# Transposing attention probabilities with VectorE 32x32 blocks and SBUF-to-SBUF DMAs instead of TensorE

## The chip, the cores and the metric

The kernel runs on one NeuronCore of a Trainium2 chip. Five engines work side by side, each through its own instructions in the order in which they were written: TensorE (PE; its weight loads are listed apart as PEld), VectorE (DVE), ScalarE (ACT), GpSimd (POOL) and SyncE (SP), which here issues every DMA. They wait for one another through semaphores. The metric is the time of one execution on the device in microseconds; the time before is the median of three runs.

## The reference

First an attention in which keys and values are averaged over groups of eight positions, then a gated feed-forward block with four weight matrices, all in float32.

```python
B, H, S, D = 8, 8, 576, 64                      # q, k, v: (B, H, S, D)
k_p = k.reshape(B, H, 72, 8, D).mean(axis=3)    # 72 pooled keys for each head
v_p = v.reshape(B, H, 72, 8, D).mean(axis=3)
scores = q @ k_p.T / sqrt(D)
attn = softmax(scores)
attn_out = attn @ v_p                           # 4608 tokens x 512
x = attn_out.transpose(0, 2, 1, 3).reshape(4608, 512)
out = (((x @ w1) * (x @ w2)) @ w3) @ w_out      # 512 -> 1024 -> 1024 -> 512
```

The kernel first multiplies w3 by w_out into one 1024 x 512 matrix, and splits values into a high and a low part, so that three (in one place four) matrix products in a shorter format give the accuracy of float32.

## The kernel before

**Chunks and tiles.** The 4608 tokens are cut into 12 chunks of 384 (`CH`). A chunk that lies in one batch element has three tiles of 128 tokens; chunks 1, 4, 7 and 10 straddle two batch elements and have four tiles of 96 (`tok_tiles`). Attention runs on tiles, the feed-forward block on whole chunks. Attention of chunk n runs beside the feed-forward block of chunk n - 1.

**One order for all engines.** Nothing is planned by costs. `at(kind, k, fn, ...)` (L599) notes a function with a slot number k; at the end (L722) the list is sorted by whole slot, then kind in the order L (loads), P (work on VectorE, ScalarE and GpSimd), M (feed-forward products), A (attention products), then the fraction of the slot, then the order of noting, and is written out. Each engine has its own instructions in just this order; the engines may be apart from one another by as much as the semaphores allow. SyncE has most of its slots empty and often runs far ahead.

**A chunk's 24 slots.** The feed-forward block of chunk m begins at slot m0. For each of eight column blocks j it takes three slots: at 3j the product with w1 (`a_mm`, L525, PSUM bank a), at 3j+1 the product with w2 (`b_mm`, bank b), and at 3j+5, so one block later, the product with the merged matrix (`out_mm`, L560). Between them, ScalarE copies a out of PSUM (`a_post`, slot 3j+1), VectorE multiplies b by it and ScalarE rounds the result to its high part gh (`b_post`, slot 3j+2), and VectorE makes the low part gl (`g_lo`, slot 3j+2.5). Banks a and b exist once each: the next `a_mm` needs `a_post`, the next `b_mm` needs `b_post`, and `out_mm` needs gl from its third matmul on. After the last block the result goes out through `out_post` (slot 27, so slot 3 of the next chunk), one of its three copies on VectorE (L572) and each followed by a store on SyncE (L575).

**A tile's attention.** `s_mm` (L404, two halves, slots s and s+1) makes the scores; `soft1` to `soft3` (slots s+1 to s+3) make exp, sum, division, and R, a small tile with the high and low parts of eight of the 72 columns; `pt_mm` and `ptr_mm` (L464, L474) transpose the probabilities E and the tile R on TensorE into PSUM, four and two 128-column pieces; one slot later `pt_post` (L486, L487) splits the result into PTh and PTl, and `ptr_post` (L491) copies PTr. When all tiles of the chunk are done, `av_mm` (L499 to L502) multiplies by the pooled values, one pair of heads at a time, and `av_post` leaves the feed-forward input xT. Attention uses three PSUM banks (tag att).

**Slots before, counted from m0 of the chunk that runs beside.** Chunk 2 and later, three tiles: s = 0, 3, 6; transposes at 5, 8, 11; `av_mm` at 15 to 18. Four tiles: s = 0, 3, 6, 9; transposes at 6, 9, 12, 15; `av_mm` at 17 to 20.

**Loads around it.** For chunk n + 1, q comes in during slots 6 to 9, one pair of heads in each (`load_q`, L265): four DMAs of 48 KB per pair, or, if chunk n + 1 straddles two batch elements, eight of 24 KB; every packet has 128 bytes. VectorE transposes q in 32x32 blocks (`tr_q`, L276, slots 15 to 18). Some chunks also load k (slots 8, 10, 12, 14; L307) and v (L343, L356). All these go through SyncE, and each of its instructions waits there until the buffer it writes is free.

Of the kernel before, what the change touches and what calls it, by code (L numbers as in the profile page):

```python
# [8 lines left out]
F32 = mybir.dt.float32  # L9
F32R = mybir.dt.float32r  # L10
# [8 lines left out]
def kernel(  # L19
# [14 lines left out]
    nc = tc.nc  # L34
# [3 lines left out]
    P = 128  # L38
# [3 lines left out]
    KR = KP - KM  # L42
# [7 lines left out]
    CH = 384  # L50
# [37 lines left out]
    def f(ap):  # L88
        return ap.bitcast(F32)
# [65 lines left out]
    def w_tiles(s):  # L155
        if s == 0:
            stage["wt"] = [t[:, i] for t, x in (
                (p1.tile([P, x, 512], I32, tag=tag, name="wt"), x)
                for tag, x in (("PTh", 3), ("PTl", 3), ("PTr", 1))) for i in range(x)]
        if s < NJ:  # L160
            stage["wo", s] = stage["wt"][s % 4], f(stage["wt"][4 + s % 3])
        stage["w3", s] = W_cell(0, 4 + s % 4, I32), W_cell(1, 4 + s % 4, F32)
# [85 lines left out]
    def tok_tiles(n):  # L248
        res = []
        for (b, s0, cnt, off) in pieces(n):  # L250
            step = 128 if cnt == 384 else 96
            for x in range(0, cnt, step):
                res.append((b, off + x, step))
        return res
# [137 lines left out]
            nc.gpsimd.tensor_tensor(  # L392
                out=VR[b % 2][rows, r // 2::2, D * par:D * par + D], in0=hi[rows], in1=m[rows], op=ALU.add)

    Et, Mt, PTh, PTl, PTr, xT = {}, {}, {}, {}, {}, {}

    Sp = {}

# [46 lines left out]
    def soft3(n, t):  # L445
        b, off, nt = tok_tiles(n)[t]
        E = Et[n, t]
        R = Rt[n, t] = p2.tile([P, NPR, 2, 2, 2, KR], F32R, tag="R", name="R")
        er = E[:nt].rearrange("p (a h) (x e) -> p a (h x) e", h=2, e=KR)[:, :, 0:18:17, :]
        for dup in range(2):  # L450
            nc.scalar.copy(out=R[:nt, :, :, dup, 0], in_=er)
        for dup in range(2):
            nc.vector.tensor_tensor(
                out=R[:nt, :, :, dup, 1], in0=er, in1=f(R[:nt, :, :, dup, 0]), op=ALU.subtract)
# [13 lines left out]
    def ptr_mm(n, t):  # L468
# [6 lines left out]
                out=rv[:, g, :nt], in_=R[:nt, g * P:(g + 1) * P], identity=ident[:nt, :nt])  # L475
        Tp[n, t, "r"] = rv

    def pt_post(n, t):
        b, off, nt = tok_tiles(n)[t]
        if t == 0:  # L480
            PTh[n] = p1.tile([P, NPR, CH], F32R, tag="PTh", name="PTh")
            PTl[n] = p1.tile([P, NPR, CH], F32R, tag="PTl", name="PTl")
            PTr[n] = p1.tile([P, 2, CH], F32R, tag="PTr", name="PTr")
        pv = Tp.pop((n, t))
        hi, lo = PTh[n][:, :, off:off + nt], PTl[n][:, :, off:off + nt]
        nc.scalar.copy(out=hi, in_=pv[:, :, :nt])  # L486
        nc.vector.tensor_tensor(out=lo, in0=pv[:, :, :nt], in1=f(hi), op=ALU.subtract)  # L487

    def ptr_post(n, t):
        b, off, nt = tok_tiles(n)[t]  # L490
        nc.scalar.copy(out=PTr[n][:, :, off:off + nt], in_=Tp.pop((n, t, "r"))[:, :, :nt])  # L491

    def av_mm(n, pr):
        ps = patt.tile([P, 512], F32, tag="att", name="att")
        for (b, s0, cnt, off) in pieces(n):
            c = slice(off, off + cnt)
            vh, vl = (vbd[b % 2][s][:, pr] for s in range(2))
            o = ps[:, c]
            nc.tensor.matmul(out=o, lhsT=vh, rhs=PTh[n][:, pr, c], start=True, stop=False)  # L499
            nc.tensor.matmul(out=o, lhsT=vh, rhs=PTl[n][:, pr, c], start=False, stop=False)  # L500
            nc.tensor.matmul(out=o, lhsT=vl, rhs=PTh[n][:, pr, c], start=False, stop=False)  # L501
            nc.tensor.matmul(out=o, lhsT=VR[b % 2][:, pr], rhs=PTr[n][:, pr // 2, c], start=False, stop=True)  # L502
        Tp[n, pr, "x"] = ps

    def av_post(n, pr):
# [93 lines left out]
    def at(kind, k, fn, *args):  # L599


        plan.append((k // 1, "LPMA".index(kind), k % 1, len(plan), fn, args))

    def plan_att(n, s_at, ds, pt_at, av_at):


        for t in range(len(tok_tiles(n))):
            for half in range(2):
                k = s_at[t] + ds * half
                at("A", k, s_mm, n, t, half)  # L610
                at("P", k + 1, soft1, n, t, half)
            at("P", k + 2, soft2, n, t)
            at("P", k + 3, soft3, n, t)
            k = pt_at[t]
            at("A", k, pt_mm, n, t)
            at("A", k, ptr_mm, n, t)
            at("P", k + 1, pt_post, n, t)
            at("P", k + 1, ptr_post, n, t)
        for pr in range(NPR):
            at("A", av_at[pr], av_mm, n, pr)  # L620
            at("P", av_at[pr] + 1, av_post, n, pr)
# [81 lines left out]
    for n in range(1, NCH):  # L703
        k = M0 + 3 * NJ * (n - 1)
        nt = len(tok_tiles(n))
        s0, pt, av = (3, 5.5, 20.5) if n == 1 else (0, 6, 17) if nt == 4 else (0, 5, 15)
        s_at = [k + s0 + 3 * t for t in range(nt)]
        plan_att(n, s_at, 1, [x + pt for x in s_at], [k + av + pr for pr in range(NPR)])
        if n == 1:
            plan_q3(n, [K0 + 8.5 + 1.5 * pr for pr in range(NPR)], [K0 + 12, K0 + 13, K0 + 15, K0 + 15.5])  # L710
        else:
            plan_q(n, k - 18, 1, k - 9, 1)
# [41 lines left out]
```

## Time and profile before

| | |
|---|---|
| median of three runs | 807.89 us (807.57 to 809.64) |
| span of the profiled execution | 803.4 us; its own time isn't listed apart, so what lies around the span is taken as the median less the span, 4.5 us |
| TensorE busy | 777.9 us, 97% |
| TensorE weight loads | 722.2 us, 90% |
| VectorE / ScalarE / GpSimd | 54% / 36% / 24% |
| mean granted TensorE clock | 0.989 |
| DMA | 62.6 MB in 106,632 packets, 73,680 of them under 512 bytes |

Busy time of TensorE overlaps itself, since matmuls are pipelined; where one group of products really gives way to the next is better read from the start of its first weight load. The chain in part 4 of the page is followed back from the last instruction. In a timeline, a row gives the start in us, the duration, the engine and line, the operation with output and inputs, and how many were merged.

### The profile page before, as it was taken

What the parts mean: (1) busy time and instruction counts of PE and PEld (TensorE: products, weight loads), DVE (VectorE), ACT (ScalarE), POOL (GpSimd) and SP (SyncE); (2) the same over time, 40 slices, a digit from 0 to 9 for tenths busy, and PEclk for the clock granted to TensorE, in tenths of its full rate; (3) what the DMA queues carried; (4) which work ended last, traced back from release to release, by engine and by line L of the source; (5) the groups of instructions that cost most, each with busy time, mean ns of one, the idle gap of its engine ahead of it and who ended that gap; (6) DMA issues with size and microseconds to landing.
All of it is one profiled execution on the core that took longest, in us unless ns stands there. A gap on an engine that the chain in (4) does not pass through costs nothing.

```text
span 803.4 us, 11625 instructions
## 1 busy us (share of the span) xinstructions
PE 777.9 (97%) x4344; PEld 722.2 (90%) x4344; DVE 431.7 (54%) x873; ACT 288.0 (36%) x727; POOL 196.1 (24%) x234
## 2 busy tenths in 40 slices
PE   7899888999999999999999999999999999999998
PEld 6677777899999999999999999999999999999997
DVE  6968989465373375374374374474454455452112
ACT  5567565332243233242242333232242332332211
POOL 2155465107007302025008102034028020000000
PEclk8999999999999999999999999999999999999999
DMA  9988960045034030062043030071143110100101
GB/s 333 267 206 217 273 145 1 1 94 123 1 72 120 27 80 1 1 143 75 1 95 109 27 67 1 17 157 44 43 85 91 53 26 1 40 1 1 40 1 39
DMA packets 106632, 62.63 MB, mean 78 GB/s; under 512 B 73680, under 2 KB 90320, under 8 KB 106576
## 3 DMA queue, kind: packets, MB, share of 16 engines
q1 hardware_dynamic: 106576, 61.89, 30.1%
q8 instruction: 34, 0.56, 0.3%
q14 instruction: 22, 0.18, 0.1%
HBM read 52.43 MB, written 9.44 MB: 77 GB/s over the span
## 4 chain that ended last, share of the span: by engine, by line
PE 85%; DVE 7%; DMA 4%; issue 2%; ACT 2%; SPq 0%; DVEq 0%
PE o L560 24%; PE a L525 24%; PE b L525 23%; PE att L404 4%; PE o L586 2%; DMA st<-in_k_dram 2%; PE att L464 2%; DVE wb L140 1%; DVE wb L148 1%; PE att L501 1%; PE att L500 1%; PE att L502 1%; PE att L499 1%; PE att L474 1%; DMA raw<-in_moe_w_out_dram 1%
## 5 line engine op out<-in xcount | busy, mean ns | idle before, releaser
L525 PE MATMUL a<-xT,hl 128*128 128x384 f32 x1152 | 223.1, 342 | 0.0
L525 PE MATMUL b<-xT,hl 128*128 128x384 f32 x1152 | 220.3, 339 | 0.4 <-DVE Wc L153 0.4
L525 PEld LDWEIGHTS a<-xT,hl 128*128 128x128 f32 x1152 | 205.0, 190 | 4.9 <-POOL hl L153 0.2
L525 PEld LDWEIGHTS b<-xT,hl 128*128 128x128 f32 x1152 | 198.7, 188 | 0.8 <-DVE Wc L153 0.8
L560 PE MATMUL o<-Wc,gh 128*128 128x512 f32 x576 | 183.6, 400 | 0.0
L560 PEld LDWEIGHTS o<-Wc,gh 128*128 128x128 f32 x576 | 105.1, 189 | 17.3
L545 DVE TENSOR_TENSOR a<-b,a 128x384 f32<-128x384 f32 x96 | 53.1, 553 | 123.5 <-PE b L525 123.5
L362 POOL TENSOR_TENSOR st<-st 72x512 f32<-72x512 f32 (+1 forms) x53 | 73.0, 1377 | 173.2 <-DMA st<-in_k_dram 161.0
L560 PE MATMUL o<-Wc,gl 128*128 128x512 f32 x288 | 114.0, 396 | 0.0
L535 ACT COPY a<-a 128x384 f32<-128x384 f32 x96 | 46.1, 480 | 179.9 <-PE a L525 160.6
L546 ACT CAST gh<-a 128x384 fp32r<-128x384 f32 x96 | 49.2, 512 | 148.4 <-DVE a L545 148.4
L551 DVE TENSOR_TENSOR gl<-a,gh 128x384 fp32r<-128x384 f32 x96 | 59.4, 619 | 35.8 <-ACT gh L546 35.4
L375 POOL TENSOR_TENSOR vbd<-vm,vbd 64x256 fp32r<-64x256 f32 x16 | 13.3, 833 | 249.8 <-ACT vbd L374 248.2
L560 PEld LDWEIGHTS o<-Wc,gl 128*128 128x128 f32 x288 | 54.1, 188 | 12.5
L511 DVE TENSOR_TENSOR xT<-att,xT 128x384 fp32r<-128x384 f32 x48 | 26.5, 556 | 70.0 <-ACT xT L510 70.0
L426 DVE TENSOR_REDUCE sm<-E 128x4 f32<-128x288 f32 (+1 forms) x70 | 31.6, 451 | 46.3 <-ACT E L425 46.3
L404 PE MATMUL att<-kbd,qT 128*128 128x144 f32 (+1 forms) x320 | 52.1, 286 | 0.2 <-ACT E L430 0.2
L420 DVE TENSOR_REDUCE mx<-att 128x4 f32<-128x288 f32 (+1 forms) x80 | 36.0, 450 | 28.8 <-PE att L404 28.7
L425 ACT ACTIVATE E<-E 128x288 f32<-128x288 f32 (+1 forms) x70 | 31.1, 445 | 55.4 <-DVE E L422 55.4
L404 PEld LDWEIGHTS att<-kbd,qT 128*128 128x128 f32 (+1 forms) x320 | 46.6, 179 | 1.1 <-ACT E L430 0.5
L586 PE MATMUL o<-hl 128*128 128x512 f32 x144 | 42.3, 430 | 3.3 <-DVE hl L177 3.3
L363 POOL TENSOR_TENSOR st<-st 72x256 f32<-72x256 f32 (+1 forms) x53 | 41.8, 789 | 4.2
(87 smaller groups left out, 806.4 us busy)
## 6 DMA issues: line engine op xcount, KB each, us to landing
raw<-in_moe_w_dram SPq DMA_DIRECT2D x32, 512.0 KB
st<-in_k_dram SPq DMA_DIRECT2D x32, 288.0 KB
out_dram<-ob SPq DMA_DIRECT2D x35, 256.0 KB
st<-in_v_dram SPq DMA_DIRECT2D x32, 256.0 KB
qs<-in_q_dram SPq DMA_DIRECT2D x128, 48.0 KB
raw<-in_moe_w_out_dram SPq DMA_DIRECT2D x8, 512.0 KB
st<-in_v_dram SPq DMA_DIRECT2D x64, 64.0 KB
qs<-in_q_dram SPq DMA_DIRECT2D x96, 24.0 KB
```

The source lines that it names most:

```text
L362: nc.gpsimd.tensor_tensor(out=t[:, :, 0:4], in0=t[:, :, 0:4], in1=t[:, :, 4:8], op=ALU.add)
L363: nc.gpsimd.tensor_tensor(out=t[:, :, 0:2], in0=t[:, :, 0:2], in1=t[:, :, 2:4], op=ALU.add)
L404: nc.tensor.matmul(out=ps[:nt, 2 * KP * j:2 * KP * (j + 1)], lhsT=qT[n][:, pr, off:off + nt], rhs=kbd[b % 2][:, pr], start=True, stop=True,)
L420: nc.vector.tensor_reduce(out=mx[:nt, hs], in_=sv, axis=AX.X, op=ALU.min)
L426: nc.vector.reduce_sum(out=sm[:nt, hs], in_=E[:nt, hs], axis=AX.X)
L525: nc.tensor.matmul(out=o, lhsT=w12[j, w][sw][:, kt * P:(kt + 1) * P], rhs=x[sx][:, kt], start=(i == 0), stop=(i == 3 * NK - 1))
L535: nc.scalar.copy(out=a, in_=gt[m, j][:, :CH])
L545: nc.vector.tensor_tensor(out=g, in0=ps[:, :CH], in1=g, op=ALU.mult)
L546: nc.scalar.copy(out=gh, in_=g)
L551: nc.vector.tensor_tensor(out=gl, in0=g, in1=f(gh), op=ALU.subtract)
L560: nc.tensor.matmul(out=oacc[m][t], lhsT=(gh, gl)[sg][:, c], rhs=W[j][sw], start=(j == 0 and i == 0), stop=(j == NJ - 1 and i == 2))
L586: nc.tensor.matmul(out=wacc[h][it], lhsT=w3t[s][sa][:, it * P:(it + 1) * P], rhs=wo[j][sb], start=(j == 0 and i == 0), stop=(j == NJ - 1 a ...
```

## The change

From chunk 2 on, `pt_mm`, `ptr_mm`, `pt_post` and `ptr_post` aren't used. In their place stand three functions. `pt_turn` (slot s+4, VectorE) transposes E and R in 32x32 blocks into a tile T of 128 x 6 x 128. `pt_move` (slot s+5, SyncE) puts the blocks in their places with DMAs from T to the tile PTx: one for each 32 tokens and each 32 of the 128 target partitions, so 16 for a tile of 128 tokens and 12 for one of 96; each moves 32 partitions x 6 x 32 numbers, 24 KB in pieces of 128 bytes. `pt_split` (slot s+9) makes PTh on ScalarE and subtracts it on VectorE, in place in the first four parts of PTx; the last two parts of PTx take the place of PTr. T and PTx have one buffer each, and R now has one in place of two. The scores begin one slot earlier (s = -1, 2, 5 and, with four tiles, 8); `av_mm` is at 17 to 20, or at 18.5 to 21.5 with four tiles. Chunks 0 and 1 keep TensorE's transposes and write to the new tiles.

```diff
     def soft3(n, t):
         b, off, nt = tok_tiles(n)[t]
         E = Et[n, t]
-        R = Rt[n, t] = p2.tile([P, NPR, 2, 2, 2, KR], F32R, tag="R", name="R")
+        R = Rt[n, t] = p1.tile([P, NPR, 2, 2, 2, KR], F32R, tag="T" if (n, t) == (0, 1) else "R", name="R")
...
+    def pt_tiles(n):
+        PTh[n] = p1.tile([P, NPR, CH], F32R, tag="PTh", name="PTh")
+        PTx[n] = p1.tile([P, NPR + 2, CH], F32R, tag="PTx", name="PTx")
+
+    def pt_turn(n, t):
+
+        b, off, nt = tok_tiles(n)[t]
+        if t == 0:
+            pt_tiles(n)
+        E = Et[n, t].rearrange("p (a h) k -> p a (h k)", h=2)
+        T = Tp[n, t] = p1.tile([P, NPR + 2, P], F32, tag="T", name="T")
+        nc.vector.transpose(out=T[:nt, :NPR], in_=E[:nt, :, KR:KR + P])
+        nc.vector.transpose(
+            out=T[:nt, NPR:].rearrange("p a c -> p (a c)"),
+            in_=f(Rt[n, t][:nt].rearrange("p a h u s e -> p (a h u s e)")))
+
+    def pt_move(n, t):
+        b, off, nt = tok_tiles(n)[t]
+        T = Tp.pop((n, t))
+        for c in range(nt // 32):
+            for g in range(4):
+                nc.sync.dma_start(
+                    out=f(PTx[n])[32 * g:32 * g + 32, :, off + 32 * c:off + 32 * c + 32],
+                    in_=T[32 * c:32 * c + 32, :, 32 * g:32 * g + 32])
+
+    def pt_split(n, t):
+        b, off, nt = tok_tiles(n)[t]
+        hi, lo = PTh[n][:, :, off:off + nt], PTx[n][:, :NPR, off:off + nt]
+        split(f(lo), hi, lo)
+
...
             at("P", k + 2, soft2, n, t)
             at("P", k + 3, soft3, n, t)
+            if n > 1:
+                at("P", k + 4, pt_turn, n, t)
+                at("L", k + 5, pt_move, n, t)
+                at("P", pt_at[t], pt_split, n, t)
+                continue
             k = pt_at[t]
             at("A", k, pt_mm, n, t)
             at("A", k, ptr_mm, n, t)
...
-        s0, pt, av = (3, 5.5, 20.5) if n == 1 else (0, 6, 17) if nt == 4 else (0, 5, 15)
+        s0, pt, av = (3, 5.5, 20.5) if n == 1 else (-1, 9, 18.5) if nt == 4 else (-1, 9, 17)
         s_at = [k + s0 + 3 * t for t in range(nt)]
         plan_att(n, s_at, 1, [x + pt for x in s_at], [k + av + pr for pr in range(NPR)])
```

More of the change, by code (lines that the diff above doesn't have):

```diff
@@ L158, in w_tiles @@
                 (p1.tile([P, x, 512], I32, tag=tag, name="wt"), x)
-                for tag, x in (("PTh", 3), ("PTl", 3), ("PTr", 1))) for i in range(x)]
+                for tag, x in (("PTh", 3), ("PTx", 4))) for i in range(x)]
         if s < NJ:
@@ L393, in prep_vr2 @@
                 out=VR[b % 2][rows, r // 2::2, D * par:D * par + D], in0=hi[rows], in1=m[rows], op=ALU.add)
-    Et, Mt, PTh, PTl, PTr, xT = {}, {}, {}, {}, {}, {}
+    Et, Mt, PTh, PTx, xT = {}, {}, {}, {}, {}
     Sp = {}
@@ L480, in pt_post @@
         if t == 0:
-            PTh[n] = p1.tile([P, NPR, CH], F32R, tag="PTh", name="PTh")
-            PTl[n] = p1.tile([P, NPR, CH], F32R, tag="PTl", name="PTl")
-            PTr[n] = p1.tile([P, 2, CH], F32R, tag="PTr", name="PTr")
+            pt_tiles(n)
         pv = Tp.pop((n, t))
-        hi, lo = PTh[n][:, :, off:off + nt], PTl[n][:, :, off:off + nt]
+        hi, lo = PTh[n][:, :, off:off + nt], PTx[n][:, :NPR, off:off + nt]
         nc.scalar.copy(out=hi, in_=pv[:, :, :nt])
@@ L490, in ptr_post @@
         b, off, nt = tok_tiles(n)[t]
-        nc.scalar.copy(out=PTr[n][:, :, off:off + nt], in_=Tp.pop((n, t, "r"))[:, :, :nt])
+        nc.scalar.copy(out=PTx[n][:, NPR:, off:off + nt], in_=Tp.pop((n, t, "r"))[:, :, :nt])
     def av_mm(n, pr):
@@ L499, in av_mm @@
             nc.tensor.matmul(out=o, lhsT=vh, rhs=PTh[n][:, pr, c], start=True, stop=False)
-            nc.tensor.matmul(out=o, lhsT=vh, rhs=PTl[n][:, pr, c], start=False, stop=False)
+            nc.tensor.matmul(out=o, lhsT=vh, rhs=PTx[n][:, pr, c], start=False, stop=False)
             nc.tensor.matmul(out=o, lhsT=vl, rhs=PTh[n][:, pr, c], start=False, stop=False)
-            nc.tensor.matmul(out=o, lhsT=VR[b % 2][:, pr], rhs=PTr[n][:, pr // 2, c], start=False, stop=True)
+            nc.tensor.matmul(out=o, lhsT=VR[b % 2][:, pr], rhs=PTx[n][:, NPR + pr // 2, c], start=False, stop=True)
         Tp[n, pr, "x"] = ps
```

## The prediction

> **What bounds the kernel now.** I read first the page's busy times and its chain of waits.
>
> ```profile
> span 803.4 us, 11625 instructions
> PE 777.9 (97%) x4344; PEld 722.2 (90%) x4344; DVE 431.7 (54%) x873; ACT 288.0 (36%) x727; POOL 196.1 (24%) x234
> PE 85%; DVE 7%; DMA 4%; issue 2%; ACT 2%; SPq 0%; DVEq 0%
> DVE a L545 <- PE b L525: 123.5, 62, 5.0
> ```
>
> TensorE holds 85% of the chain, and VectorE mostly waits for it (fourth row, from the list of waits: 123.5 us before the product with b). So each TensorE instruction taken out is worth its own time, as long as nothing else gets late. What it is worth, and when TensorE needs what, stands in the timeline of weight loads beside chunk 3 (three tiles, 128 tokens), and at the end for a tile of 96:
>
> ```profile
> 401.83 2.17 PEld L525 LDWEIGHTS a<-xT,hl 128*128 128x128 f32 x12
> 403.99 0.60 PEld L404 LDWEIGHTS att<-kbd,qT 128*128 128x128 f32 x4
> 404.53 2.05 PEld L525 LDWEIGHTS b<-xT,hl 128*128 128x128 f32 x12
> ...
> 409.08 0.59 PEld L464 LDWEIGHTS att<-ident,E 128*128 128x128 f32 x4
> 409.64 0.25 PEld L474 LDWEIGHTS att<-ident,R 128*128 128x128 f32 x2
> 409.86 2.06 PEld L525 LDWEIGHTS a<-xT,hl 128*128 128x128 f32 x12
> ...
> 433.03 0.19 PEld L499 LDWEIGHTS att<-PTh,vbd 128*128 128x128 f32 x1
> ...
> 433.74 2.10 PEld L525 LDWEIGHTS b<-xT,hl 128*128 128x128 f32 x12
> ...
> 436.52 0.36 PEld L560 LDWEIGHTS o<-Wc,gh 128*128 128x128 f32 x2
> 436.93 0.19 PEld L560 LDWEIGHTS o<-Wc,gl 128*128 128x128 f32 x1
> ...
> 469.51 0.48 PEld L464 LDWEIGHTS att<-ident,E 96*128 96x128 f32 x4
> 470.10 0.49 PEld L404 LDWEIGHTS att<-kbd,qT 128*96 128x96 f32 x4
> ```
>
> **What it removes.** The six transposes of a 128-token tile take TensorE from 409.08 to 409.86, 0.78 us, those of a 96-token tile from 469.51 to 470.10, 0.59 us. Chunks 2 to 11 have 21 tiles of 128 (seven chunks) and 12 of 96 (chunks 4, 7, 10): 21 x 0.78 + 12 x 0.59 = 23.4 us. ScalarE loses the copies of PTr. The split stays, now out of SBUF; I keep its times. None of that is on the chain.
>
> **What it adds.** VectorE transposes 768 numbers per partition in two instructions. ScalarE's and VectorE's rows, grouped by shape:
>
> ```profile
> L276 DVE STREAM_TRANSPOSE qT<-qs 128x384 f32<-128x384 f32 x40 | 22.7, 568 | 0.0
> L486 ACT CAST PTh<-att 128x512 fp32r<-128x512 f32 x24 | 14.0, 583 | 17.3 <-PE att L464 17.3
> L487 DVE TENSOR_TENSOR PTl<-att,PTh 128x512 fp32r<-128x512 f32 x24 | 16.6, 690 | 12.5 <-ACT PTh L486 12.5
> L551 DVE TENSOR_TENSOR gl<-a,gh 128x384 fp32r<-128x384 f32 x96 | 59.4, 619 | 35.8 <-ACT gh L546 35.4
> ```
>
> 768 is twice 384, so 2 x 0.568 = 1.14 us per tile. VectorE is busy for 54% of the span, so its idle time covers that; without this cover it would be 33 x 1.14 = 38 us. R with one buffer, and scores a slot earlier, I cost at nothing: `pt_turn` has read R two slots before the next tile's R is written, and TensorE does the same scores. If R did make ScalarE wait, it would be for one `pt_turn`, 1.14 us a tile.
>
> The real cost is SyncE's. It must issue 16 (or 12) DMAs per tile, 48 per chunk in both kinds of chunk. Nothing in this trace moves SBUF to SBUF; SyncE's own timeline shows what issues cost otherwise:
>
> ```profile
> 404.05 11.89 SPq L265 DMA_DIRECT2D qs<-in_q_dram  x24
> ...
> 416.44 3.76 SPq L265 DMA_DIRECT2D qs<-in_q_dram  x8
> 420.30 0.79 SPq L307 DMA_DIRECT2D st<-in_k_dram  x2
> ...
> 436.50 5.40 SPq L356 DMA_DIRECT2D st<-in_v_dram  x8
> ...
> 462.30 9.54 SPq L265 DMA_DIRECT2D qs<-in_q_dram  x16
> ...
> 169.68 5.60 SPq L265 DMA_DIRECT2D qs<-in_q_dram  x11
> ```
>
> An issue costs 0.395 us at the least (k, 0.79 for two) and 0.675 at the most (v, 5.40 for eight). The nearest is q of chunk 4: 24 KB each, the same 32 partitions, six pieces and 128 bytes as the moves; 11.89/24 = 0.495 and 3.76/8 = 0.47. I take 0.485; for the 48 KB form 5.60/11 = 0.51. To see when the last lands, the DMA view of 462 to 474 us (40 slices of 0.3 us):
>
> ```profile
> qs<-in_q_dram SPq DMA_DIRECT2D x16, 48.0 KB
> DMA  1999999847548284654839457200008386472000
> ```
>
> SyncE ends the sixteenth at 462.30 + 9.54 = 471.84, so began it about 471.35; packets cease in slice 37, near 473.1: 1.75 us from issue to landing. A tile of 128 thus occupies SyncE for 16 x 0.485 = 7.76 us, and has landed 15 x 0.485 + 1.75 = 9.0 us after the first issue; a tile of 96 takes 5.8 and 7.1 us. TensorE reaches a next tile after three slots, some 7 us. And T has one buffer: the next `pt_turn` waits, on VectorE, for all 16 landings, with `soft1` of the next tile and `b_post` queued behind it; `pt_split` waits for them on ScalarE, with `a_post` behind it, and on VectorE with `g_lo` behind it.
>
> **The chain of one chunk.** Zero is the start of slot 3 (401.83 above). TensorE wants the fifth gl at its third matmul of slot 17: 436.93 - 401.83 = 35.1 us before the change, less three tiles' transposes (2.3), two `av_mm` that move behind it (433.03 to 433.74, 0.71 each) and one half of scores (403.99 to 404.53, 0.54): 30.8 us. `g_lo` of block 4 (slot 14.5) stands behind `pt_split` of tile 2 (slot 14) on VectorE. When is that ready? `pt_turn` 0 stands behind `out_post`'s copy:
>
> ```profile
> 402.47 0.68 DVE L572 COPY ob<-o 128x512 f32<-128x512 f32 x1
> ```
>
> so it ends near 403.15 + 1.14, at 2.5. SyncE's order is move 0, q pair 0, move 1, q pairs 1 to 3, move 2.
>
> Chunks 2, 5, 8 (next q: four 48 KB issues, 2.04 us, per pair): move 0 is issued 2.55 to 10.3 and landed at 11.6; q to 12.35; `pt_turn` 1 runs 11.6 to 12.75; move 1 12.75 to 20.5; q to 26.6; move 2 26.6 to 34.4, landed 35.65. Then the split's 0.58 + 0.69, `g_lo`'s 0.6 and 0.3 us that I allow for three handoffs: 37.8. Late by 7.0 us.
>
> Chunks 3, 6, 9 (next q: eight 24 KB issues, 3.9 us, per pair): q to 14.2; move 1 to 21.95; q to 33.6; move 2 to 41.35, landed 42.6; gl at 44.75. Late by 13.95.
>
> Chunks 4, 7, 10: move 0 2.5 to 8.35, landed 9.6; q to 10.4; `pt_turn` 1 to 10.7; move 1 to 16.55; q to 22.65; move 2 to 28.5, landed 29.75; `pt_turn` 3, planned for slot 12 (some 21), runs 29.75 to 30.85; move 3 to 36.7, landed 38.0, split done 39.3. `av_mm` wants it at 36.0: slot 17 starts at 30.4 and two more halves of scores (1.1), then come two products of some 2.2. Late by 3.3.
>
> Chunk 11 (no q after it): landings at 11.6, 21.8, 32.0; gl at 34.15. Late by 3.4.
>
> Sum of the stalls: 3 x 7.0 + 3 x 13.95 + 3 x 3.3 + 3.4 = 76.1 us. TensorE catches up nothing, since it is the bound between the stalls; SyncE does, as it now stands idle before the stores of a chunk for up to 54.7 us:
>
> ```profile
> SPq L575 <- ACT ob L574: 439.3, 12, 54.7
> ```
>
> The q and k loads that now stand behind moves still come in time: the last q pair is issued by 33.6, and `tr_q` of it stands in slot 18. Net +76.1 - 23.4 = +52.7: a span of 856.1, and with the 4.5 us between this span (803.4) and the median of the runs (807.89), 861 us.
>
> **Bounds.** With 0.395 us an issue, the same steps give stalls of 2.85, 9.8, 0 and 0: 38.0 in all, +14.6, 822 us. With 0.675: 15.75, 23, 11.8 and 11.8: 163.5, +140, 948 us. The middle price is kept because its DMAs have the same form and size as the moves; that the source is SBUF instead of DRAM is the open point.
>
> **Rivals.** *Hidden, faster.* If the issues cost little, only 23.4 us of TensorE go: 784.5. The place is the wait for move 2. By the steps above gl is ready at 15.4 + 46c (chunks 2, 5, 8) and 22 + 47c (3, 6, 9) for an issue price c, against 30.8. All is hidden for c below 0.19; the stalls equal the gain near c = 0.35, and below that the change wins. For it: VectorE's and the DMA engines' free time. Against it: no group of issues above is below 0.395. The Trainium skill, DMA: Bandwidth & Descriptors, Rules for kernel authors, says to issue a DMA early and wait late, so that its fixed cost overlaps compute; the five slots between `pt_turn` and `pt_split` do that for one tile, and by this rule alone the time would be this rival's. No row here bears it out for 48 issues in a row.
>
> *Cheap issues, slightly slower.* c between 0.36 and 0.43, as for k: by the same two lines, 812 to 837.
>
> *Packets, not issues, set the pace.* In the stretch of the 24 issues the DMA engines are busy a third of the time:
>
> ```profile
> 408.00:410.00 2.00, 2.00 (x14) 1.70 (x13) 1.45 (x4) 0.78 (x3) 0.00 (x0) 1.00 0.32 51
> ```
>
> 0.32 of 0.485 us is 0.155 us of packets per DMA. Were SBUF to SBUF packets over three times as slow, they would outlast the issue; at four times, 0.62 us a DMA, so some 921 us. The Trainium skill, DMA: Bandwidth & Descriptors, Specifications, says that below 512 bytes a DMA engine does read-modify-write; a doubling by that would stay hidden at a share of 0.64.
>
> **How the numbers follow.** A difference under 0.3% (2.4 us) can't be told from none. The forecast (c from 0.43 to 0.6, 837 to 911 us) gets 0.63; cheap issues 0.13; dearer issues or packets (over 911) 0.09; hidden or nearly so, 784 to 805, 0.12; a draw, with c at 0.35, 0.03. Slower is 0.63 + 0.13 + 0.09 = 0.85. The range, 806 to 925, leaves out the faster cases, part of the draw and the far end.
>
> **What would show it.** In the changed kernel: SyncE rows of 16 moves in about 7.8 us, back to back; VectorE idle before its transposes of tiles 1 and 2, ended by a DMA from T; ScalarE idle before the split of the last tile, 5 us and more; TensorE's gaps at the out product of slot 17, about 7 us beside chunks 2, 5, 8 and 14 beside chunks 3, 6, 9; granted clock unchanged. It would be wrong if an issue from SBUF costs under 0.35 us, if VectorE doesn't wait for T, or if TensorE's gaps stand elsewhere.

## The result, and the profile after

The changed kernel takes 977.64 us (971.9 to 980.32), the kernel before, run beside it, 808.45: a ratio of 1.211, 95% interval 1.205 to 1.218. The prediction had the sign and the bound right and the size wrong: 861 us, with a range to 925. The profiled execution has a span of 974.4 us where the prediction's sum gave 856.1, so 118 us have to be explained.

The page of the changed kernel (busy times, granted clock, chain of waits):

```profile
PE 814.7 (84%) x4146; PEld 741.6 (76%) x4146; DVE 451.0 (46%) x939; ACT 279.2 (29%) x694; POOL 193.1 (20%) x234
PEclk8999999889978989978977997987997897998999
PE 37%; SPq 32%; DVE 14%; DMA 8%; issue 5%; ACT 3%; DVEq 0%; ACTq 0%
```

TensorE held 85% of the chain before; now it holds 37% and SyncE's queue (SPq) 32%, of which 28 points are the one line that issues the moves. VectorE's busy time grows by 19 us only (451.0 against 431.7). The granted clock (PEclk, in tenths of full speed) falls in patches.

Its list of waits:

```profile
DVE T L489 <- DMA PTx<-T: 137.5, 23, 11.6
DVE PTx L153 <- ACT PTh L152: 129.2, 33, 14.1
PEld b L553 <- DVE a L573: 82.5, 18, 9.7
ACT PTh L152 <- DMA PTx<-T: 81.6, 10, 12.9
PEld o L588 <- DVE gl L579: 56.7, 15, 8.7
```

Before, VectorE waited for TensorE's b, and TensorE for hardly anything. Now the reverse has appeared: TensorE waits for VectorE's a and gl, VectorE for T or for ScalarE's PTh, and both for the moves. The prediction named these waits, but it looked for TensorE's gaps at gl and `av_mm` alone. The larger share stands before the product with b, at slots 10 and 13 of a chunk with three tiles: `b_post` is queued on VectorE behind the turn of the next tile, and that turn waits for T.

Chunk by chunk: the table of windows, before and after. Each row runs from the first product with w1 of one chunk to that of the next; the rows are those in which attention of chunks 3 and 4 runs beside (the same table has 58.11 us for chunk 2 and 57.94 for chunk 11). Columns: window, length, busy time of PE, PEld, DVE, ACT, POOL with counts, granted clock, DMA share, GB/s. Before, without a gap in TensorE's busy time:

```profile
218.31:276.56 58.25, 58.25 (x328) 54.92 (x326) 28.76 (x62) 19.12 (x47) 21.17 (x27) 1.00 0.29 75
276.56:336.31 59.75, 59.75 (x353) 56.38 (x352) 31.46 (x74) 19.39 (x51) 6.65 (x9) 1.00 0.12 27
```

After, chunks 2, 3, 4 and 11; where the busy time of PE is shorter than the window, TensorE stands idle:

```profile
163.26:239.05 75.79, 62.99 (x311) 58.08 (x310) 29.61 (x67) 16.98 (x40) 15.02 (x18) 0.89 0.36 73
239.05:321.35 82.30, 61.62 (x310) 56.46 (x309) 30.43 (x67) 18.32 (x44) 20.83 (x27) 0.90 0.33 68
321.35:391.83 70.48, 62.02 (x331) 56.19 (x330) 34.77 (x81) 18.82 (x47) 5.89 (x9) 0.95 0.21 40
849.74:917.77 68.03, 58.81 (x303) 54.25 (x302) 27.64 (x63) 15.91 (x37) 0.00 (x0) 0.95 0.14 30
```

The four kinds of chunk grow by 17.7, 24.1, 10.7 and 10.1 us, and TensorE, which had no gap, stands idle for 12.8, 20.7, 8.5 and 9.2 us. The prediction's net figures were 7.0 - 2.3, 13.95 - 2.3, 3.3 - 2.4 and 3.4 - 2.3, so 4.7, 11.6, 0.9 and 1.1: the order of the kinds is right, and each is about 9 to 13 us too small. The window after the last of these is as before (56.6 us both times): nothing is lost there, where there are no moves.

The chain that the prediction worked out, in the chunk that was hit worst, chunk 3. SyncE's own timeline, after:

```profile
250.11 10.44 SPq L499 DMA_DIRECT2D PTx<-T  x16
260.59 7.85 SPq L265 DMA_DIRECT2D qs<-in_q_dram  x16
268.55 10.33 SPq L499 DMA_DIRECT2D PTx<-T  x16
278.93 3.98 SPq L265 DMA_DIRECT2D qs<-in_q_dram  x8
283.01 0.36 SPq L307 DMA_DIRECT2D st<-in_k_dram  x1
283.41 4.28 SPq L265 DMA_DIRECT2D qs<-in_q_dram  x8
...
288.24 10.72 SPq L499 DMA_DIRECT2D PTx<-T  x16
```

From 250.11 to 298.96 the queue issues without a break. Sixteen moves take 10.3 us, 0.65 us each (10.33/16), where the prediction had 7.76. What follows the last move stands in three timelines of the same kernel: TensorE's weight loads (their first row is this chunk's zero, the start of slot 3), then ScalarE, then VectorE:

```profile
246.31 2.05 PEld L553 LDWEIGHTS a<-xT,hl 128*128 128x128 f32 x12
...
282.00 3.70 PEld L553 LDWEIGHTS b<-xT,hl 128*128 128x128 f32 x12 [9.46 <-DVE a L573]
...
302.20 0.29 PEld L588 LDWEIGHTS o<-Wc,gl 128*128 128x128 f32 x1 [8.70 <-DVE gl L579]
```

```profile
300.34 0.62 ACT L152 CAST PTh<-PTx 128x512 fp32r<-128x512 f32 x1 [12.91 <-DMA PTx<-T]
```

```profile
249.64 0.40 DVE L490 STREAM_TRANSPOSE T<-R 128x256 f32<-128x256 f32 x1
...
280.47 0.71 DVE L489 STREAM_TRANSPOSE T<-E 128x512 f32<-128x512 f32 x1 [11.39 <-DMA PTx<-T]
...
281.43 0.52 DVE L573 TENSOR_TENSOR a<-b,a 128x384 f32<-128x384 f32 x1
...
300.99 0.69 DVE L153 TENSOR_TENSOR PTx<-PTx,PTh 128x512 fp32r<-128x512 f32 x1 [14.11 <-ACT PTh L152]
```

The end is the chain as forecast: last move, landing, split on ScalarE and VectorE, the fifth gl, the out product of slot 17, which waited 8.70 us. But TensorE gets gl at 302.20 - 246.31 = 55.9 us, not 44.75. And it had stood 9.46 us before that, at 282.00: the turn of tile 2 waited 11.39 us for the moves of tile 1, and the product of b and a (281.43) stood behind it.

### The profile page after: what moved, and what is told of

It is laid out like the page before. It is cut to its first block, busy times and chain, and to the rows that moved or that the text cites. A ratio compares the mean times of both kernels' runs of the same rounds, so it can differ in the third digit from the quotient of the medians.

```text
span 974.4 us, 11953 instructions
## 1 busy us (share of the span) xinstructions
PE 814.7 (84%) x4146; PEld 741.6 (76%) x4146; DVE 451.0 (46%) x939; ACT 279.2 (29%) x694; POOL 193.1 (20%) x234
## 4 chain that ended last, share of the span: by engine, by line
PE 37%; SPq 32%; DVE 14%; DMA 8%; issue 5%; ACT 3%; DVEq 0%; ACTq 0%
SPq L499 28%; PE o L588 11%; PE b L553 9%; PE a L553 9%; DMA PTx<-T 5%; SPq L265 3%; PE o L614 2%; DMA qs<-in_q_dram 2%; DVE T L489 1%; PE att L404 1%; DVE mx L420 1%; DVE E L422 1%; ACT E L425 1%; DVE sm L426 1%; PE att L528 1%
## 5 line engine op out<-in xcount | busy, mean ns | idle before, releaser
L553 PE MATMUL b<-xT,hl 128*128 128x384 f32 x1152 | 247.1, 367 | 77.4 <-DVE a L573 76.8
L553 PEld LDWEIGHTS b<-xT,hl 128*128 128x128 f32 x1152 | 221.1, 208 | 83.4 <-DVE a L573 82.5
L553 PE MATMUL a<-xT,hl 128*128 128x384 f32 x1152 | 226.2, 345 | 1.1 <-ACT a L563 1.1
L588 PE MATMUL o<-Wc,gh 128*128 128x512 f32 x576 | 192.7, 417 | 1.1 <-ACT gh L574 1.1
L588 PE MATMUL o<-Wc,gl 128*128 128x512 f32 x288 | 122.6, 426 | 49.7 <-DVE gl L579 49.7
L588 PEld LDWEIGHTS o<-Wc,gh 128*128 128x128 f32 x576 | 115.0, 203 | 20.8 <-ACT gh L574 2.5
L588 PEld LDWEIGHTS o<-Wc,gl 128*128 128x128 f32 x288 | 58.3, 202 | 70.0 <-DVE gl L579 56.7
L574 ACT CAST gh<-a 128x384 fp32r<-128x384 f32 x96 | 49.2, 512 | 215.9 <-DVE a L573 215.9
L489 DVE STREAM_TRANSPOSE T<-E 128x512 f32<-128x512 f32 (+1 forms) x33 | 23.3, 707 | 137.5 <-DMA PTx<-T 137.5
L153 DVE TENSOR_TENSOR PTx<-PTx,PTh 128x512 fp32r<-128x512 f32 (+1 forms) x33 | 21.4, 649 | 129.2 <-ACT PTh L152 129.2
L579 DVE TENSOR_TENSOR gl<-a,gh 128x384 fp32r<-128x384 f32 x96 | 56.6, 589 | 15.5 <-ACT gh L574 14.8
```

Of the source, the lines that this page charges most:

```text
L553: nc.tensor.matmul(out=o, lhsT=w12[j, w][sw][:, kt * P:(kt + 1) * P], rhs=x[sx][:, kt], start=(i == 0), stop=(i == 3 * NK - 1))
L574: nc.scalar.copy(out=gh, in_=g)
L579: nc.vector.tensor_tensor(out=gl, in0=g, in1=f(gh), op=ALU.subtract)
L588: nc.tensor.matmul(out=oacc[m][t], lhsT=(gh, gl)[sg][:, c], rhs=W[j][sw], start=(j == 0 and i == 0), stop=(j == NJ - 1 and i == 2))
```

## The experiments

Theory 1: SyncE's issue time is the whole cause; an issue whose source is SBUF costs more than one from DRAM, so every chain is longer than worked out. Theory 2: the half clock after each gap (the row at 302.20 takes 0.29 us; the same load takes 0.19 in the prediction's timeline) adds a second loss of its own. A third candidate is T, which exists once, so that VectorE waits for it.

### What sets the price of an issue (e1_ladder)

Extra DMAs at the end of the kernel, in groups that differ in one thing.

```diff
+    def ladder():
...
+        for c, g in cg:                       # the move's own form
+            nc.sync.dma_start(out=d0[r(g), :, r(c)], in_=src[r(c), :, r(g)])
+        for c, g in cg:                       # the same pieces from DRAM
+            nc.sync.dma_start(out=d1[r(g), :, r(c)], in_=q[0, g, 192 * c:192 * c + 192, 0:32].rearrange("(n t) e -> t n e", t=32))
...
+    at("L", M0 + 3 * NJ * (NCH - 1) + 6, ladder)
```

> The changed kernel, with a ladder of extra DMAs while the last chunk's feed-forward block runs and SyncE has nothing else to do; they copy a tile of zeros to buffers that nobody reads. Seven groups on SyncE's queue: the move's own form (SBUF to SBUF, 32 partitions, six pieces of 128 bytes), the same destination form with q in DRAM as source, three pieces, one piece, six pieces that stay on their partitions, one piece on 128 partitions, six pieces on 128 partitions; and the move's form once more on GpSimd's queue. Read per group: time from one issue to the next. Theory 1 (the source decides): the move's form 0.65 us, from DRAM 0.48 us, and piece count and partitions change little. Theory 2 (descriptors decide): the move's form and the form from DRAM cost the same, three pieces about half of 0.65 us, one piece less still. The total should stay within 1% of the changed kernel's 977.6 us, since the ladder stands where SyncE is idle.

The timeline of SyncE in this kernel, the move's form:

```profile
932.37 7.74 SPq L551 DMA_DIRECT2D ld<-lsrc  x12
```

The view by line gives the durations of single instructions (min/median/max in ns): the move's form, the same 24 KB in the same pieces from DRAM, one piece a partition in place of six, six pieces on all 128 partitions, and the move's form on GpSimd:

```profile
L551 SPq DMA_DIRECT2D ld<-lsrc x12: 597/604/609, 932.4 to 939.5; - x12
L553 SPq DMA_DIRECT2D ld<-in_q_dram x12: 439/440/1517, 940.1 to 946.7; - x12
L557 SPq DMA_DIRECT2D ld<-lsrc x12: 562/588/590, 955.2 to 962.1; - x12
L565 SPq DMA_DIRECT2D ld<-lsrc x8: 630/664/678, 978.9 to 983.9; - x8
L563 POOL DMA_DIRECT2D ld<-lsrc x12: 565/566/705, 919.1 to 925.4; - x12
```

The group from DRAM holds one straggler of 1517 ns; its median is 440. To a duration comes the gap to the next issue, 7.74/12 - 0.604 = 0.04 us; from the start of one move to the start of the next the median of the changed kernel is 0.648 us. So the same pieces cost about 0.48 us from DRAM and 0.648 from SBUF. The number of pieces hardly counts (588 ns for one, 604 for six), nor do four times the partitions (664 ns for 96 KB against 604 for 24). For this form the memory that is read sets the difference. It isn't the whole price of an issue: k and v come from DRAM too, and the prediction's rows have them at 0.395 and 0.675 us. The moves of the changed kernel have the same 604 ns as their median. The whole took 991.35 us in its one execution, 1.4% more than the changed kernel, where I had expected 1% at most: the last stores stand behind the ladder.

### Fewer issues between the moves (e3_q_early)

The next chunk's q comes ten slots earlier, before the moves, in place of between them.

```diff
-            plan_q(n, k - 18, 1, k - 9, 1)
+            plan_q(n, k - 18 if n == 2 else k - 28, 1, k - 9, 1)
```

> The changed kernel, with the loads of the next chunk's q ten slots earlier (from chunk 3's on), so that they no longer stand between the moves in SyncE's queue. Theory 1 (SyncE's queue is the limit, 0.648 us an issue): by the prediction's steps gl would be ready at 41.9 us after the start of slot 3 in every three-tile chunk instead of 45.6 or 52; chunks 2, 5, 8 gain about 7 us each, chunks 3, 6, 9 about 14, chunks 4, 7, 10 about 4: some 74 us less, about 903 us. Theory 2 (VectorE's transposes and their waits for T are the limit, the queue is not): within 10 us of 977.

Measured 922.18 us, 1.143 (1.140 to 1.146): 55 us less, by nothing but the order of one queue, though 19 short of what I expected. SyncE beside chunk 3 shows where the rest sits:

```profile
245.49 23.39 SPq L499 DMA_DIRECT2D PTx<-T  x32
```

Two moves take 23.39 us where 32 issues of 0.65 are 20.7: between them the queue now stands still for 2.7 us, the landing of the first and the turn of the second. With q out of the way it is T, not the queue, that makes the second move late.

### A second T alone (e4_two_T)

```diff
-        T = Tp[n, t] = p1.tile([P, NPR + 2, P], F32, tag="T", name="T")
+        T = Tp[n, t] = tp.tile([P, NPR + 2, P], F32, tag="T2", name="T")
```

The pool tp has two buffers; for its space the staging buffers go from four to three.

> The changed kernel with two buffers for T in place of one (and three instead of four staging buffers for k and v, to make room). VectorE then need not wait for the moves of the tile before. Theory 1 (SyncE's queue is the limit): chunks 2, 3, 5, 6, 8, 9 stay as they are, chunks 4, 7, 10 gain 2.6 us each, chunk 11 5 us: about 964 us. Theory 2 (the single buffer T, on which VectorE waits 137 us in all, is the limit): most of these 137 us go, 840 to 880 us.

Measured 965.5 us, 1.197 (1.194 to 1.200). It gives 12 us, about where theory 1 has it: the chunk windows of chunks 2 and 3 stay at 76.6 and 82.5 us, that of chunk 4 falls by 2.6 and that of chunk 11 by 2.8. The list of VectorE's waits has no row for T any more, and the time has moved one instruction down. TensorE's list has no row for b any more either; its wait for gl is now as long as those for b and gl together were (82.5 + 56.7 = 139.2 us):

```profile
DVE PTx L154 <- ACT PTh L153: 239.1, 26, 17.8
PEld o L592 <- DVE gl L583: 142.8, 24, 12.1
```

For the most part, the 137.5 us for T were where waiting was done, not what caused it. Beside chunks 2 and 3, where the queue has no break, a second buffer changes nothing.

### The clock (e5_warm)

Filler transposes of the identity, into one of attention's three PSUM banks, keep TensorE at work in the gaps beside chunks 2, 3, 5, 6, 8 and 9.

```diff
+        if n in (2, 5, 8):
+            for x, c in ((9, 30), (12, 34), (16, 55)):
+                at("A", k + x, warm, c)
+        if n in (3, 6, 9):
+            for x, c in ((9, 26), (12, 80), (16, 74)):
+                at("A", k + x, warm, c)
```

> The changed kernel with dummy transposes of the identity on TensorE just ahead of the products that stall beside chunks 2, 3, 5, 6, 8 and 9, about as many as fill each stall (3 to 9 us each, 12 to 19 us a chunk). Theory 1 (after a stall TensorE is granted half its clock for some 7 us and so loses 4 to 6 us more per chunk, beyond the stall): the granted clock rises from 0.918 to above 0.95, and the time falls by 3 to 5 us a chunk, 18 to 30 us in all, to about 950 us. Theory 2 (the half clock falls into time in which TensorE waits anyway): the clock rises, the time stays at 977 or grows by the dummies that outlast their stalls.

The clock rises from 0.918 to 0.963 over the span, beside chunk 3 from 0.90 to 0.98, and the time stays: 979.79 us, 1.215 (1.212 to 1.219). The window of chunk 3 in this kernel:

```profile
236.65:320.90 84.25, 78.52 (x491) 73.76 (x490) 29.83 (x67) 18.33 (x44) 20.69 (x27) 0.98 0.32 66
```

Most of the half clock falls into time in which TensorE would have waited anyway. Only what follows a chunk's last gap is a loss: beside chunk 3, 3.1 us at a clock of 0.50 (the rows are in the last section), some 1.6 us a chunk and 16 us in all, an estimate from that chunk. The fillers bear it out beside chunks 2, 5 and 8, where the stretch from TensorE's first gl of slot 17 to the end of the chunk falls from 19.3 to 19.8 us to 17.7 to 17.8. But there gl itself comes 0.7 to 1.3 us later, and beside chunks 3, 6 and 9 a gap of 3.2 to 4.0 us is left at slot 17, and the half clock after it. So the fillers brought no gain.

### Half of the moves from another queue (e6_pool_queue)

```diff
-                nc.sync.dma_start(
+                (nc.sync if g < 2 else nc.gpsimd).dma_start(
```

> The changed kernel, with the moves to the upper 64 of the 128 target partitions (half of them) issued by GpSimd instead of SyncE. The ladder had GpSimd's issues at 0.557 us against 0.648 us on SyncE. Theory 1 (SyncE's queue is the limit): SyncE issues 24 moves per chunk in place of 48, its chain shrinks by 24 x 0.648 = 15.6 us per chunk; the stalls go in chunks 2, 4, 5, 7, 8, 10 and 11, and 6 to 8 us each are left in chunks 3, 6, 9: 805 to 825 us. Theory 2 (the DMA engines or VectorE's transposes are the limit): within 3% of 977. Open is how far GpSimd's own work, its sums of k and v, is put off by its issues.

Measured 854.37 us, 1.059 (1.056 to 1.062): 123 us less with the same 480 DMAs, the same bytes and the same single T. This is the strongest single piece of evidence that issuing on one queue was the bound, not the transfers. The Trainium skill, DMA: Bandwidth & Descriptors, Rules for kernel authors, says that spreading DMAs over the issuing engines brings no bandwidth and only saves sequencer issue time. The trace agrees, and here that "only" is worth 123 us.

It missed the 805 to 825 that I expected, at two places. SyncE's rows and GpSimd's, first beside chunk 3, then beside chunk 4:

```profile
259.77 5.13 SPq L499 DMA_DIRECT2D PTx<-T  x8
...
317.10 14.88 SPq L499 DMA_DIRECT2D PTx<-T  x12
```

```profile
252.66 4.46 POOL L499 DMA_DIRECT2D PTx<-T  x8 [2.31 <-DVE T L490]
...
321.86 0.45 POOL L364 TENSOR_TENSOR vrm<-st 128x128 f32<-128x128 f32 x1
322.38 3.35 POOL L499 DMA_DIRECT2D PTx<-T  x6
```

Beside chunks 3, 6 and 9 (67.7 to 68.6 us a window, 58.25 before) the late half is still SyncE's: it begins its last eight moves at 259.77, after q and k, while GpSimd began its own at 252.66. Beside chunks 4, 7 and 10 (64.7 to 65.0, 59.75 before) it is GpSimd's: its moves of tile 2 wait in program order behind the additions that average v, until 322.38, while SyncE's began at 317.10.

### One tile of each chunk, with time to spare (e7_one_tile)

Only tile 0 goes by moves, its split is at slot 12, all other tiles keep TensorE's transposes, and scores and `av_mm` go back almost to the old slots.

```diff
-            if n > 1:
+            if n > 1 and t == 0:
                 at("P", k + 4, pt_turn, n, t)
...
-        s0, pt, av = (3, 5.5, 20.5) if n == 1 else (-1, 9, 18.5) if nt == 4 else (-1, 9, 17)
+        s0, pt, av = (3, 5.5, 20.5) if n == 1 else (-1, 6, 17) if nt == 4 else (-1, 6, 15)
...
+        if n > 1:
+            pt_at[0] = k + 12
```

> Only tile 0 of each chunk from 2 on is transposed by VectorE and moved by DMAs, its split is put off to slot 12; the other tiles use TensorE as before the change, at the slots they had. SyncE then issues 16 moves per chunk, 10.4 us, landed about 16 us after the start of slot 3, and the split is wanted at about 20. Theory 1 (only the queue's length costs): nothing stalls, and TensorE saves 7 x 0.78 + 3 x 0.59 = 7.2 us: 800 us, ratio 0.991. Theory 2 (VectorE's transposes, or traffic beside them, cost by themselves): no faster than before, 807 or more.

Measured 800.09 us, 0.992 (0.990 to 0.994), as expected: 0.8% under the kernel before, little, but clear of the interval. The mechanism itself works: ten tiles' transposes leave TensorE, and nothing else gets late. The window of chunk 3:

```profile
218.62:276.24 57.62, 57.62 (x323) 54.30 (x322) 29.90 (x63) 18.79 (x46) 21.47 (x27) 1.00 0.37 83
```

0.63 us less than before (58.25), no idle time, full clock.

### All tiles, with later use (e8_late)

q early, two T, splits at slots 11, 15, 20 (9, 13, 16, 20 for four tiles), `av_mm` from 20.2.

```diff
-        s0, pt, av = (3, 5.5, 20.5) if n == 1 else (-1, 9, 18.5) if nt == 4 else (-1, 9, 17)
+        s0, pt, av = (3, 5.5, 20.5) if n == 1 else (-1, 9, 20.2)
...
+        pt_at = [x + pt for x in s_at] if n == 1 else [k + x for x in ((9, 13, 16, 20) if nt == 4 else (11, 15, 20))]
```

> All tiles moved as in the change, but with q loaded ten slots earlier, two buffers for T (three staging buffers for k and v), splits at slots 11, 15 and 20 (9, 13, 16 and 20 with four tiles) and the products with the pooled values at slots 20 to 23. SyncE issues 48 moves per chunk without a break, 31.1 us from 3.8 us after the start of slot 3, landed at 36; the last split is due about 37.5. Theory 1 (the chain of SyncE's issues against the due times is all there is): no stall is left, 23.4 us of TensorE are saved: 785 us, up to 795 if the late products crowd the chunk's end. Theory 2 (48 moves cost something that no order hides, VectorE's waits or the clock): above 820.

Measured 833.44 us, 1.034 (1.030 to 1.038); a miss. The four-tile chunks came out without a gap, at 58.1 to 58.4 us against 59.75, chunk 11 at 56.05 against 57.94. The chunks with loads of k did not (61.5 to 65.5). SyncE beside chunk 3:

```profile
237.27 21.47 SPq L503 DMA_DIRECT2D PTx<-T  x32
258.84 0.94 SPq L308 DMA_DIRECT2D st<-in_k_dram  x2
```

The k loads, due in slots 8 to 14, stand behind 32 moves, the other two of the four behind all 48. They are few issues, but TensorE waits for what GpSimd makes of them:

```profile
PEld att L329 <- POOL km L365: 17.8, 10, 2.4
```

The splits are late as well, though less: TensorE waits 7.8 us for them, in six waits. The wait had moved to the next thing in the queue. That there are three staging buffers instead of four may add to it; the two were not told apart.

### Fewer, larger DMAs by way of DRAM (e9_dram, e10_dram_q)

If an issue costs about the same whatever it moves, five can do the work of sixteen: T goes out to a DRAM buffer with one DMA for each 32 tokens, in the transposed order, and comes back with one for the whole tile.

```diff
+            nc.sync.dma_start(
+                out=S[:, :, :, 32 * c:32 * c + 32].rearrange("g i a j -> i a g j"),
+                in_=T[32 * c:32 * c + 32].rearrange("i a (g j) -> i a g j", g=4))
...
+    def pt_back(n, t):
+        b, off, nt = tok_tiles(n)[t]
+        nc.sync.dma_start(
+            out=f(PTx[n])[:, :, off:off + nt],
+            in_=Tp.pop((n, t, "s")).rearrange("g i a j -> (g i) a j"))
```

> The changed kernel with its slots as they are, but each tile goes from T to a buffer in DRAM and back: four DMAs of 32 partitions write it there in transposed order (98 KB each), and one slot later one DMA of 128 partitions reads it to PTx. Five issues per tile in place of 16, 3.1 us at 0.648 us. Theory 1 (number of issues): T is read about 5 us after its transposes end, the tile is back about 8 us after them if a DRAM landing takes 2 us each way, due after 9 us; no stall or little, 785 to 795 us. Theory 2 (bytes or small packets are what the queue pays for): an issue of 768 pieces costs four times one of 192, no gain on the changed kernel, 950 us or more.

Measured 852.05 us, 1.055 (1.051 to 1.060): 126 us less than the changed kernel, with one T and q where it was. But it isn't under the kernel before, and far from the 785 to 795 that I expected. SyncE beside chunk 3:

```profile
235.68 2.73 SPq L500 DMA_DIRECT2D S<-T  x4
240.31 0.58 SPq L506 DMA_DIRECT2D PTx<-S  x1
240.94 7.89 SPq L266 DMA_DIRECT2D qs<-in_q_dram  x16
248.94 2.68 SPq L500 DMA_DIRECT2D S<-T  x4
251.66 4.03 SPq L266 DMA_DIRECT2D qs<-in_q_dram  x8
...
256.19 1.48 SPq L506 DMA_DIRECT2D PTx<-S  x1
```

A tile now occupies SyncE for 2.73 + 0.58 = 3.3 us instead of 10.4, but the q loads, by now the longer part, still stand between one tile's way out and its way back. So the next kernel has both edits, the way through DRAM and q ten slots earlier.

> The way through DRAM (five DMAs per tile) and, as well, q loaded ten slots earlier. In the run through DRAM alone, chunk 11, which has no q behind it, took 55.4 us in place of 57.9 before the change, and the other chunks stalled where eight or sixteen q loads stood between a tile's DMAs. Theory 1 (order and number of SyncE's issues are all that cost): those stalls go, every chunk gains what chunk 11 gains, about 23 us less than before: 785 us, ratio 0.972, or up to 792 if the loads of k and v still stand in the way. Theory 2 (a landing in DRAM with its wait on SyncE costs by itself): chunks with other loads stay 4 us and more over, 820 us or more.

Measured 803.49 us, 0.995 (0.993 to 0.998), where I expected 785 to 792. The window of chunk 4:

```profile
276.72:338.59 61.87, 59.62 (x331) 55.37 (x330) 34.65 (x81) 18.88 (x47) 10.89 (x15) 0.97 0.34 75
```

By the same table chunk 11 has the gain (55.38 us for 57.94), and so have chunks 2 and 3 (56.39 and 56.80 us for 58.11 and 58.25); the chunks of 96-token tiles are 2.1 us longer than before.

### Two tiles by moves (e11_two_tiles)

As with one tile, but tiles 0 and 1, splits at slots 12 and 17, `av_mm` from 18, and q early.

```diff
-            if n > 1:
+            if n > 1 and t < 2:
...
+        if n > 1:
+            pt_at[:2] = k + 12, k + 17
```

> Tiles 0 and 1 of each chunk from 2 on moved as in the change, q ten slots earlier, splits at slots 12 and 17, the other tiles on TensorE, products with the pooled values from slot 18. SyncE issues 32 moves (24 with four tiles), the second tile landed 28 us after the start of slot 3, its split due at 31. Theory 1 (the chain of issues against the due times): nothing stalls, 14 tiles of 128 and 6 of 96 save 14.5 us: 793 us, ratio 0.982. Theory 2 (something else grows with the number of moves, as loads of k put off): above 800, the time of one tile.

Measured 843.74 us, 1.046 (1.044 to 1.049); a clear miss, and the reason is T:

```profile
DVE T L489 <- DMA PTx<-T: 62.3, 10, 9.7
```

Ten waits, one in each chunk: three slots (7 us) lie between the turns of tile 0 and tile 1, and a move takes 10.3 us and its landing. VectorE stands at the second turn, and TensorE's bank b behind it. With one tile there is no second turn to wait; with two, spreading the splits does not help, since it is the turns that are too close.

### What was left in the way through DRAM (e12_dram_vr, e13_before_vr)

With the way through DRAM and q early the four-tile chunks were still longer than before. ScalarE's waits beside chunk 4 in that kernel (276 to 338 us):

```profile
ACT vrh L382 <- POOL vrm L365: 3.6, 1, 3.6
```

ScalarE waits for GpSimd's vrm, part of the next values; the split of tile 1 is queued behind on ScalarE, VectorE waits 4.9 us for that split, and turn 3 waits behind it. The same wait of ScalarE stands in the kernel before, 21.4 us in six, with nothing urgent behind it. Both kernels were given the same edit, `prep_vr` two slots later:

```diff
-            plan_v(b, k + 1, k + 3, k + 6, k + 9, k + 10)
+            plan_v(b, k + 1, k + 3, k + 6, k + 9, k + 12)
```

> The way through DRAM with the early q loads, and the rest of the values (prep_vr) prepared two slots later; nothing left out. In the run before it the chunks of 96-token tiles took 61.9 us in place of 59.8, and their trace shows why: ScalarE stands 3.6 us at prep_vr's first copy, since GpSimd has not finished vrm; the split of tile 1 is queued behind it on ScalarE, VectorE waits 4.9 us for that split, and the turn of tile 3, the last move and the out product of slot 17 all come late, 2.2 us of idle TensorE and 3.4 us at half clock. Theory (order on ScalarE is what is left): without that wait these chunks fall to some 57.5, so 3 x 4.3 = 13 us off: 788 to 793 us, 0.977 to 0.983 of before, and TensorE has no gap over 0.5 us beside chunks 4, 7, 10. Rival (the fourth tile's move is late by itself, one T and 3 slots): the chunks stay at 61 to 62, 800 to 805 us.

> The kernel before with prep_vr two slots later and nothing else, as the counterpart of the run with the way through DRAM. Theory: the 3.6 us wait of ScalarE is in the kernel before too (21.4 us in 6 waits), but nothing that TensorE needs stands behind it there, so the time stays at 0.997 to 1.003 of before. Rival: the wait costs the kernel before as well, some 2 us in each of three or more chunks: 0.985 to 0.995.

With the way through DRAM: 790.63 us, 0.978 (0.975 to 0.981). The kernel before with this edit: 807.82 us, 1.000 (0.998 to 1.002), although its wait for vrm falls from 21.4 to 12.5 us. Chunk 4 has lost its gap:

```profile
279.02:336.80 57.78, 57.78 (x331) 54.50 (x330) 35.57 (x81) 19.06 (x47) 10.91 (x15) 1.00 0.37 81
```

57.78 us against 61.87 in the run before it and 59.75 in the kernel before. Beside chunk 3 a gap of 1.65 us at the gl of slot 17 is left, and the window, 58.55 us, gains nothing (58.25 before). As a whole this version beats both kernels, and the idea of the change, all transposes off TensorE, is what it gains by: the same slot edit alone gains nothing, and the windows shrink by about what the transposes took. The kernel before was not run with q ten slots earlier; beside chunks 3 and 4 it has no gap of TensorE that this could close.

## Why the prediction was wrong

**What bounds the kernel: right. Where TensorE would stall: half right.** The queue, the turn, the landing, the split and the last product that waits were named, and the trace shows them in this order. But the sign that the prediction gave, gaps at the out product of slot 17 of about 7 and 14 us, isn't what stands there: 4.5 to 6.4 us beside chunks 2, 5, 8 and 8.3 to 8.7 beside 3, 6, 9, and in all TensorE waits longer for b (82.5 us) than for gl (56.7). Beside chunks 4, 7, 10 the gaps stand at b and at the out product of slot 14; at `av_mm` there is one, of 1.7 us, beside chunk 4. The prediction had `b_post` queued behind a waiting turn and gave it no gap. The sum doesn't suffer from this, since what TensorE loses early it need not wait for later: with two T's the waits for b are gone and the window of chunk 3 is as long as before (82.5 us).

**What it removes, 23.4 us: about right, as far as it can be seen.** Where nothing waits, in the last run through DRAM, a window loses 2.56 us in chunk 11 (57.94 to 55.38, three tiles of 128; the prediction had 3 x 0.78 = 2.34), 1.97 in chunk 4 (2.36) and 1.74 in chunk 2.

**The price of an issue: the step that failed.** "The middle price is kept because its DMAs have the same form and size as the moves; that the source is SBUF instead of DRAM is the open point." The open point decided: 0.648 us, not 0.485. By the prediction's own two lines, 15.4 + 46c and 22 + 47c, gl comes at 45.2 and 52.45 us, 14.4 and 21.7 late; the other two kinds of chunk hold 45 issues and come 0.163 x 45 = 7.3 us later, 10.6 and 10.7. Together 3 x 14.4 + 3 x 21.7 + 3 x 10.6 + 10.7 = 150.8 us of stalls in place of 76.1, so 75 of the missing 118 us. This price lay within the bounds given (0.395 to 0.675), nearer to v's than to q's. The upper one was tied to v by its price alone; nothing in the trace of before could show why v should be the nearer row, and nothing spoke against it.

**A misreading of the plan: the second failed step.** The prediction put `pt_turn` and `pt_move`, and the description ahead of it `soft2` and `soft3` as well, one slot too early. In `plan_att` these lines stand behind the loop over the two halves and use its last k, so for the changed chunks the turn is at s+5 and the move at s+6. Turn 0 therefore ended at 250.04 - 246.31 = 3.7 us, not 2.5, and SyncE's order is move 0, q pairs 0 and 1, move 1, q pairs 2 and 3, move 2, as the timeline shows (16 q issues after the first move where the prediction had one pair of 8), with k loads between the later pairs (0.72 us here), which the chain left out. Together with the dearer q (7.85/16 = 0.49 us and a little more) the last move of chunk 3 ends at 52.65 us where the prediction's steps at 0.648 give 41.35 + 48 x 0.163 = 49.2. Of these 3.5 us, 1.25 are the later start (250.11 - 246.31 = 3.8 instead of 2.55); the changed order alone costs nothing here, since the queue has no break either way. Over all chunks, TensorE gets the fifth gl at 48.5 to 49.1 us beside chunks 2, 5, 8 and at 55.6 to 56.1 beside 3, 6, 9, so 3.2 to 3.9 us after the 45.2 and 52.45 above. (The rows that the prediction calls those beside chunk 3, with q of chunk 4, stand beside chunk 6, with q of chunk 7. They are of the same kind, so no term changes.)

**"Granted clock unchanged": wrong, and small.** After a chunk's last gap some 1.6 us are lost, about 16 us in all. With the 75 us from the price that leaves about 27 us, some 2.7 us a chunk, for the later start and the extra issues. This division is worked out, not measured edit by edit.

**The landing: about right.** From the end of the last issue to ScalarE's start 300.34 - 298.96 = 1.38 us; the prediction's 1.75 from the start of the issue is 1.27 from its end.

**T with one buffer: half right.** The prediction had turns wait for T on the critical path. In the chunks with the most q it is SyncE that is late and T only the place of the wait; a second T gained 12 us, all of it elsewhere. T becomes the bound once the queue is relieved (q early, two tiles).

**The rivals.** *Hidden* is false for the kernel as changed, but true for one tile a chunk, and nearly so for all tiles once five issues replace sixteen, q comes earlier and `prep_vr` later: 790.63 us against this rival's 784.5. *Cheap issues* is false. *Packets set the pace* is false: four times the bytes in one issue cost a tenth more, and a second queue with the same packets took 123 us away. *Dearer issues*, the case over 911 us, held; it had been given a chance of 0.09 together with slow packets, which was too little, since three prices stood in the trace and nothing but likeness of form spoke for the middle one. And the range's upper end, 925, would have had to be the 948 of the dear price, with something for the terms that had been left out; even 948 was too low.

## What to carry to other kernels

Where a change replaces compute by many small DMAs, count the issues on one queue and everything that stands between them, and price them by a row that is like them in source memory and in shape; where the trace has none, carry the whole spread of its issue prices into the range. When issue time binds, put more into each issue or use a second queue, and move foreign loads out from between a producer's and a consumer's DMAs; a second buffer behind a full queue gains little. After each wait that is removed, look at what comes next in an in-order queue: here it was q, then T, then k on SyncE, then a copy of v on ScalarE.

## What the runs showed of the hardware that I had not expected

- An issue on SyncE costs 604 ns plus 0.04 from SBUF and 440 ns plus 0.04 from DRAM, with the same pieces; one or six pieces and 32 or 128 partitions make little difference (588 to 664 ns). On GpSimd the move's form takes 566 ns. Why SBUF is dearer no run here shows, nor why an issue for k takes 0.395 us and one for v 0.675, both from DRAM.
- In TensorE's gap of 8.7 us beside chunk 3 the granted clock is 1.00 for the first 4.4 us and falls to half while the gap still lasts (0.50 from 298.5 to 302.1). After the gap it stays at half for 3.1 us of work:

```profile
294.00:298.40 4.40, 0.00 (x0) 0.00 (x0) 0.00 (x0) 0.00 (x0) 0.17 (x1) 1.00 0.24 39
302.20:305.30 3.10, 3.10 (x7) 2.49 (x8) 2.86 (x5) 0.51 (x1) 1.76 (x2) 0.50 1.07 174
```

- From 305.4 us on the clock is 1.00 again by itself, and keeping it up by filler work gained nothing while another queue was the bound.
- A way through DRAM and back, with two landings in it, was faster for the kernel than SBUF to SBUF, 852.05 against 977.64 us, since it takes five issues a tile and not sixteen.
